# Modulation rows on GpSimd's queue, w1's first operands made ahead of the folds, and seven buffer pairs for comparisons in an FNet and mixer-MLP kernel

## The chip, the cores and the metric

The kernel runs on one core of a Trainium2 chip. The metric is the device time of one execution in microseconds (us), the median of several runs. Engines: TensorE (PE, its weight loads PEld), VectorE (DVE), ScalarE (ACT), GpSimd (POOL) and SyncE (SP); SP, ACT and POOL each issue DMA transfers from a queue of their own. On-chip memory is SBUF (128 partitions) and eight PSUM banks of 128 x 512 f32, into which PE writes.

## The reference

All is f32, with 2048 tokens of 1024 features and d_ff 3584.

```python
mod = (_silu(c) @ w_mod).reshape(c.shape[0], 6, 1, -1)
sa, ca, ga, sb, cb, gb = ...
h = _layernorm(x) * (1 + ca) + sa
# FNet: real part of a 2-D DFT, as products with given matrices
a = einsum("bsd,ed->bse", h, dft_hid_re); b = einsum("bsd,ed->bse", h, dft_hid_im)
y = einsum("ts,bse->bte", dft_seq_re, a) - einsum("ts,bse->bte", dft_seq_im, b)
x = x + ga * y
h = _layernorm(x) * (1 + cb) + sb
u = _layernorm(h)
x = x + gb * (gelu(u @ w1 + b1) @ w2 + b2)
```

The inputs are x, the four DFT matrices, w1, b1, w2, b2, the condition c and w_mod (1024 x 6144).

## The kernel before, in words

Matmuls of the DFT and of the MLP run in f16 as three passes of a high and a low half ("split": ACT makes the high half at L2340, VectorE the low half at L2350 or L2352 and w1's combined half at L2365). The function `fast` uses symmetries of DFT matrices, and it compares the matrices that it was given with those symmetries while the MLP runs; if a comparison fails, `general` computes everything again.

The stages of `fast` in order:

1. Modulation columns (sa and ca): eight loads of w_mod (1 MB each, L2457, SP), products on PE (L2500) and on VectorE (L2489 and L2491, into the sum MACC). The result is a row in PSUM. ACT copies it to SBUF, and 32 products of one column each (L2544) turn it into columns; L2551 to L2555 finish them ("mod").
2. LN1: for each of 16 tiles of x statistics (L2582, VectorE) and normalization (L2603 and L2604, ACT), then transposes on PE (L2619) in four groups over all eight banks, and from there the modulated halves (L2637, ACT) and their folds (L2641 and L2642, VectorE). The folded operands are split again (L2690 and after).
3. The hidden DFT, 297 matmuls (L2874, "hid"), in units whose results ACT and VectorE split. Among them stand the rows: ga, sb, cb and gb are wanted as rows of 1024 on all partitions, so each of four rows is a sum over eight 512 KB pieces of w_mod, loaded by SP (L2812) into a ring of three and used by two matmuls each (L2818) in banks 6 and 7. Three of the rows are then copied within SBUF to their place (L2904).
4. The sequence DFT (L2947 and L2959, "P" and "Q"), then x + ga * y, the second and third normalization (L3013 to L3045), transposes (L3063) and splits of the MLP's left operand. Its matrices are loaded by L2763 ("cop"). w1's first two groups of columns are loaded in this stage (L3309), their norms taken (L3152, an all-reduce on GpSimd at L3164), split, and stored for later blocks (L3254).
5. The MLP: 28 groups GEMM3 (L3438, 84 matmuls each, evicted by L3460, L3464, L3457) and 14 GEMM4 (L3547, 168 matmuls each, evicted and summed by L3593; the last two by L3587). From the middle on the 148 comparisons run beside them: each loads two 128 x 512 pieces on GpSimd's queue (L3369, or gathered at L3362) into one of three buffer pairs, VectorE subtracts (L3352), and ACT squares and sums (L3345). The verdict (L3429 to L3433, with an all-reduce on GpSimd at L3430) adds the sums; the program's last branch reads it.

Every engine runs its instructions in order, and that order is made before the launch by a planner: `add` and `push` append tasks with an engine, a cost, dependencies and a due time to a stream; `pick` takes the next task from the stream with the earliest due time that can start, and `need`, `force` and `emitted` put a named task and all that stands ahead of it out at once. So an edit of a due time, a dependency or a cost moves instructions on several engines. Of the names in the diff: "wru" is the use of a row load by PE, "tpd" the end of the transposes of an LN1 block, "n" the normalization of a tile, "cru" the use of a ring buffer of sequence operands, "rowe" the copy of a finished row by ACT, FP the planner's cost of an f32 matmul.

## Time and profile before

| | us |
|---|---|
| median of 3 runs | 1569.62 (1568.48 to 1572.24) |
| profiled execution | 1573.34 |
| its span | 1571.5 |
| PE busy | 1319.7 (84%) |
| DVE busy | 1121.2 (71%) |
| ACT busy | 738.6 (47%) |
| POOL busy | 254.4 (16%) |

Times in the profile count from the span's start. A row of a timeline gives the start, the busy time, the engine, the line, the operation with its operands, the number of instructions run together (x), and in brackets how long the engine had been idle before and what released it. A row of a group gives the busy time, the mean of one instruction in ns, and the idle time before such instructions with what ended most of it. A window's row gives busy times of each engine in a stretch. An f32 matmul leaves two records, so a row's 64 matmuls show as 128.

### The profile page before, as it was taken

What the parts mean: (1) busy time and instruction counts of PE and PEld (TensorE: products, weight loads), DVE (VectorE), ACT (ScalarE), POOL (GpSimd) and SP (SyncE); (2) the same over time, 40 slices, a digit from 0 to 9 for tenths busy, and PEclk for the clock granted to TensorE, in tenths of its full rate; (3) what the DMA queues carried; (4) which work ended last, traced back from release to release, by engine and by line L of the source; (5) the groups of instructions that cost most, each with busy time, mean ns of one, the idle gap of its engine ahead of it and who ended that gap; (6) DMA issues with size and microseconds to landing.
All of it is one profiled execution on the core that took longest, in us unless ns stands there. A gap on an engine that the chain in (4) does not pass through costs nothing.

```text
span 1571.5 us, 17349 instructions
## 1 busy us (share of the span) xinstructions
PE 1319.7 (84%) x6081; PEld 635.8 (40%) x6081; DVE 1121.2 (71%) x1723; ACT 738.6 (47%) x1173; POOL 254.4 (16%) x415
## 2 busy tenths in 40 slices
PE   6515899946428899999999999979999999999980
PEld 2413345624313344444444444434444444444430
DVE  6875413898984779989898899635576857676872
ACT  2724112667666568464655535135535353434412
POOL 1000000000124000000000000133243233225233
PEclk9555999968658999999999999989999999999995
DMA  9313753243479846263534437588677777675564
GB/s 371 112 27 94 245 181 136 81 141 107 152 247 197 247 148 221 98 224 122 204 137 168 149 140 312 163 276 302 230 236 260 247 227 254 224 263 184 203 147 164
DMA packets 107337, 300.18 MB, mean 191 GB/s; under 512 B 13644, under 2 KB 13644, under 8 KB 105320
## 3 DMA queue, kind: packets, MB, share of 16 engines
q1 hardware_dynamic: 75080, 194.06, 36.0%
q0 software_dynamic: 32160, 104.93, 21.6%
q8 instruction: 49, 0.80, 0.2%
q14 instruction: 48, 0.39, 0.1%
HBM read 212.43 MB, written 84.93 MB: 189 GB/s over the span
## 4 chain that ended last, share of the span: by engine, by line
PE 66%; DVE 12%; DMA 9%; issue 7%; ACT 3%; POOL 2%; SPq 1%; DVEq 0%; POOLq 0%; ACTq 0%
PE ps L3438 28%; PE ps L3547 27%; PE ps L2818 3%; DMA arena<-in_wm_dram 3%; PE ps L2874 3%; DMA arena<-in_cre_dram 2%; PE ps L2947 2%; PE ps L2959 1%; DMA arena<-in_w_dram 1%; PE ps L2500 1%; DVE arena L2365 1%; DVE arena L2350 1%; DVE arena L2352 1%; DMA arena<-in_dim_dram 1%; DMA arena<-in_cim_dram,idxs 1%
## 5 line engine op out<-in xcount | busy, mean ns | idle before, releaser
L3438 PE MATMUL ps<-arena 128*128 128x512 f16 x2352 | 521.3, 384 | 19.5 <-ACT arena L3460 16.7
L3547 PE MATMUL ps<-arena 128*128 128x512 f16 x2352 | 515.2, 381 | 12.3 <-DVE arena L3593 7.7
L3438 PEld LDWEIGHTS <-arena 128*128 128x128 f16 x2352 | 232.7, 99 | 305.7 <-issue 35.0
L3547 PEld LDWEIGHTS <-arena 128*128 128x128 f16 x2352 | 231.2, 98 | 294.0 <-issue 19.6
L3593 DVE SCALAR_TENSOR_TENSOR arena<-ps,i4c,arena 128x1024 f32<-128x1024 f32 x179 | 229.4, 1282 | 58.8 <-PE ps L3547 55.7
L3345 ACT ACTIVATE arena<-arena 128x512 f32<-128x512 f32 (+5 forms) x148 | 91.5, 619 | 191.1 <-DVE arena L3352 125.1
L2365 DVE TENSOR_TENSOR arena<-arena 128x512 f32<-128x512 f32 (+1 forms) x228 | 171.5, 754 | 5.8 <-ACT arena L3067 1.1
L2340 ACT ACTIVATE arena<-arena,shc 128x512 f16<-128x512 f32 (+1 forms) x115 | 116.6, 1016 | 93.5 <-DVE arena L2365 57.4
L2352 DVE SCALAR_TENSOR_TENSOR arena<-arena,shc 128x512 f16<-128x512 f32 (+1 forms) x115 | 129.0, 1123 | 33.1 <-ACT arena L2340 32.7
L3352 DVE TENSOR_TENSOR arena<-arena 128x256 f32<-128x256 f32 x240 | 92.3, 422 | 73.0 <-DMA arena<-in_cre_dram 38.6
L3457 ACT ACTIVATE arena<-arena,b1s,i1c 128x512 f32<-128x512 f32 x84 | 68.3, 814 | 139.0 <-DVE arena L3464 138.8
L3464 DVE TENSOR_TENSOR arena<-arena,ps 128x512 f32<-128x512 f32 x84 | 57.5, 685 | 69.0 <-PE ps L3438 68.4
L2340 ACT ACTIVATE arena<-arena,s1c 128x512 f16<-128x512 f32 (+1 forms) x70 | 60.5, 885 | 53.8 <-DVE arena L2365 40.0
L2947 PE MATMUL ps<-arena 128*128 128x256 f16 (+3 forms) x400 | 55.9, 304 | 29.7 <-DVE arena L2974 29.5
L3164 POOL PARTITION_ALL_REDUCE sums<-sums x21 | 12.8, 609 | 402.8 <-DVE sums L3160 398.0
L3369 POOL DMA_DIRECT2D arena<-in_cim_dram x99 | 54.2, 548 | 135.6 <-ACT arena L3345 133.2
L3369 POOL DMA_DIRECT2D arena<-in_cre_dram x99 | 54.3, 548 | 126.0 <-ACT arena L3345 117.5
L2619 PE MATMUL ps<-ident,arena 128*128 128x128 f32 x128 | 26.5, 378 | 53.7 <-ACT arena L2603 52.6
L2352 DVE SCALAR_TENSOR_TENSOR arena<-arena,s1c 128x512 f16<-128x512 f32 (+1 forms) x70 | 66.3, 958 | 7.1 <-ACT arena L2340 7.1
L3063 PE MATMUL ps<-ident,arena 128*128 128x128 f32 x128 | 24.7, 357 | 54.4 <-ACT arena L3053 42.8
L2818 PE MATMUL ps<-arena,scol 128*128 128x512 f32 x128 | 63.4, 640 | 8.3 <-DMA arena<-in_wm_dram 7.1
L3460 ACT ACTIVATE arena<-ps 128x512 f32<-128x512 f32 x84 | 49.5, 589 | 36.0 <-PE ps L3438 35.9
(187 smaller groups left out, 1285.4 us busy)
## 6 DMA issues: line engine op xcount, KB each, us to landing
...
```

The lines of the kernel that those rows point to most:

```text
L2340: act.activation(o[m][0], q(j), AF.Copy, **sc)
L2352: dve.scalar_tensor_tensor(o[m][1], q(j), scale, o[m][0], op0=ALU.mult, op1=ALU.subtract)
L2365: dve.tensor_tensor(q(d), q(a), q(b), op=op)
L2818: pe.matmul(bank(6 + h), scol[:, k : k + 1].to_broadcast([P, P]), FA(o + 512 * h, (1, 512)), start=k == 0, stop=k == 7,)
L2947: pe.matmul(PA(pb + o, (1, w)), l, r, start=n == 0, stop=n == len(mm_) - 1)
L3345: f = lambda: act.activation(sq(a), sq(a), AF.Square, accum_out=csum[0:pn, n : n + 1])
L3352: dve.tensor_tensor(a[:, o::2], a[:, o::2], b[:, o::2], op=op)
L3369: return lambda t: gp.dma_start(t[0:pn], v)
L3438: pe.matmul(ps.rearrange("p (k t) -> p k t", k=4), w1c[:, m, s, a, d * P : (d + 1) * P], zc(m)[:, b, :, d, :], start=(start and d == 0 and ...
L3457: act.activation(dst, src, AF.Gelu_apprx_tanh, scale=inv, bias=b1s[:, 2 * p + j : 2 * p + j + 1])
L3547: pe.matmul(t[:, j], hidc[:, c_, m, a, k * P : (k + 1) * P], w2c[:, m, c_, w], start=(start and c_ == 0 and n == 0), stop=(c_ == 1 and n = ...
L3593: lambda: dve.scalar_tensor_tensor(dst, ps[b], inv, dst, op0=ALU.mult, op1=ALU.add), kp[b],
```

## The change

It does seven things.

1. The 32 row loads (and that of b2) go from SP's queue to GpSimd's, and the row matmuls from behind LN1 to among its transposes: their due time is 45 + 12 n in place of 60. They have banks 6 and 7 to themselves and a ring of their own in the memory that holds w1's stored halves before (first loads wait for those stores). Row results go straight to their place, and the three copies at L2904 go.
2. LN1's transposes, the special columns' and the hid units share three pairs of banks in turn (`pair`), each transposed unit followed by its fold.
3. The columns: the row is copied by ACT and VectorE together, one DMA spreads it over 16 partitions, one transpose turns it, and two small products stay.
4. w1's first two groups are loaded by eight 256 KB loads ahead of w_mod, normed and split in the modulation and LN1 stages, stored by GpSimd's queue, and loaded again as 14 pieces by SP late in the hid stage and after.
5. The loads of the sequence operands (from the third on) wait for the use of row load 23, and x tiles 12 to 15 are loaded after the first row in program order.
6. Comparisons have seven buffer pairs instead of three. All of them, with the verdict, are put out before GEMM3(27); two loads of partial outputs (`load_kept`) move from after GEMM4(7) to there.
7. The planner's cost of an f32 matmul goes from 0.85 to 0.5, and addresses move.

Core of the diff:

```diff
--- before.py
+++ after.py
@@ -2049,23 +2049,24 @@
         return mk([P, n], F32, tag, bufs)
 
 
-    X0, X4, NR = 0, 29920, 4160
+    X0, X4, NR = 0, 29920, 51200
     EO, WM2, MACC, ROW, ONES = 9344, 9344, 25792, 27840, 34048
     AR, CL = 2052, 1026
     SPB = (38912, 40968)
-    DRAW = 47168
-    CRING = (42000, 49224, 50248)
-    RTMP, RFIN, WRING, GBT = (0, 1024, 2048), (51296, 52320, 53344), (3072, 4096, 5120), 6144
-    QS = (7168, 54368)
-    Y0, W0, ZT0 = 8192, 12288, 16384
+    DRAW = 47120
+    CRING = (41996, 49176, 50200)
+    ROWS = (51264, 52288, 53312)
+    WRING, GBT = ((34656, 35680, 36704), (0, 1024, 2048)), 3072
+    QS = (54852, 54336)
+    Y0, W0, ZT0 = 8832, 12928, 17024
 
     HOP, HC = 51584, 8256
-    COP = (86144, 69632)
-    AOP, AC = (94336, 77824), 4112
-    DOP, SPOP, DSP, ASP, CSP = 102592, 106752, 108832, 109888, 110944
+    COP = (86048, 69632)
+    AOP, AC = (94240, 77824), 4112
+    DOP, SPOP, DSP, ASP, CSP = 8320, 12448, 14528, 15584, 16640
 
     def junk2(key):
...
+    for g in range(2):
+        for n in (1, 2, 0, 3):
+            load(("raw1", g, n), lambda g=g, n=n: sp.dma_start(raw1(g, n), w1[g, :, PLACE.index(n), :]), cost=0.7)
     for k in range(8):
         load(("wm", k), lambda k=k: sp.dma_start(wm2(k), wm[:, k, 0 : 2 * D]), cost=2.75)
...
-        key = load(("cr", n), lambda: f(o), [("cru", n - 3)] if n > 2 else [])
+        key = load(("cr", n), lambda: f(o), ([("cru", n - 3)] if n > 2 else []) + [("wru", 23), ("tpd", 3), ("n", 15)] * (n > 1))
...
-        act.activation(
-            FA(ROW + 257, (1024, 2), (512, 2), (1, 255), pn=1), PA(MB + 511, (1024, 2), (512, 2), (-1, 255), pn=1), AF.Copy
+        act.activation(rspec[0:1], PA(MB, (1024, 2), (256, 4), pn=1), AF.Copy)
+
+    def rows_out2():
+        dve.tensor_copy(
+            FA(ROW + 257, (1024, 2), (512, 2), (1, 255), pn=1), PA(MB + 511, (1024, 2), (512, 2), (-1, 255), pn=1)
         )
-        act.activation(rspec[0:1], PA(MB, (1024, 2), (256, 4), pn=1), AF.Copy)
+
+    def rows_spread():
+        act.dma_start(FA(MACC, (1, 128), pn=16), FA(ROW, (128, 16), (1, 128), pn=1))
 
     def cols():
+        pe.transpose(PA(MB, (1, 16)), FA(MACC, (1, 128), pn=16), ident[0:16, 0:16])
         for cs in range(2):
-            for g in range(4):
-                for j in range(2):
-                    n = (cs * 4 + g) * 2 + j
-                    pe.matmul(
-                        PA(MB + n, (1, 1)), FA(ROW + 1024 * cs + 256 * g + 128 * j, (1, 128), pn=1), ones[0:1, 0:1],
-                        start=True, stop=True,
-                    )
             pe.matmul(PA(MB + 16 + cs, (1, 1), pn=4), rspec[0:1, cs], ones[0:1, 0:1], start=True, stop=True)
...
+    add("modm", "dve", 1.1, rows_out2, [("mp", 7)], "rowd", 1.0)
     add("modm", "dve", 3.2, rows_max, [("mp", 7)], "max", 1.0)
-    add("modr", "act", 3.0, rows_out, [("mp", 7)], "rowc", 1.0)
-    add("modp", "pe", 4.5, cols, ["rowc", "max"], "cols", 1.0)
+    add("modr", "act", 1.2, rows_out, [("mp", 7)], "rowc", 1.0)
+    add("modr", "act", 0.1, rows_spread, ["rowc", "rowd"], "rows16", 1.0)
+    add("modp", "pe", 2.5, cols, ["rows16", "max"], "cols", 1.0)
     add("modm", "dve", 0.8, cols_out, ["cols", "max"], "mod", 1.0)
...
-    GB = {0: (0, 1), 3: (2, 3), 1: (4, 5), 2: (6, 7)}
-    lastbank = {}
+    last = {0: [], 1: [], 2: ["mod"]}
+    nunit = [0]
+
+    def pair():
+        nunit[0] += 1
+        return (nunit[0] - 1) % 3
 
...
+                ks = [
+                    add("lnt", "pe", 0.75, lambda g=g, bk=bk, turn=turn: turn(g, bk), deps + last[s], None, due)
+                    for g, bk in ((ga_, ba), (gd_, bd))
+                ]
...
+                k2 = add("lnd", "dve", 1.5, fold, [k1, ks[1]], ("d1", bt, j, base), 1.6)
+                last[s] = [k1, k2]
...
     def row(n, j):
         for k in range(ND):
             m = ND * n + k
-            o = WRING[m % 3]
-            l = load(
-                ("wr", m), lambda o=o, k=k, j=j: sp.dma_start(FA(o, (1, 1024)), wm[:, k, j * D : (j + 1) * D]),
-                [("wru", m - 3)] if m > 2 else [("tpd", 3), ("n", 15)], stream="ld",
-            )
+            o = WRING[m > 23][m % 3]
+            was = [("wru", m - 3)] if m > 2 else [("w1s", 1, q) for q in range(7)]
+            if 24 <= m < 27:
+                was += [("tpd", 3), ("n", 15)]
+
+            def f(o=o, k=k, j=j, m=m):
+                if m < 3:
+                    need("st_w1s")
+                gp.dma_start(FA(o, (1, 1024)), wm[:, k, j * D : (j + 1) * D])
+
+            l = add("rowl", "st", 0.0, f, was, ("wr", m))
 
             def f(k=k, o=o):
                 for h in range(2):
@@ -2822,30 +2831,43 @@
 
             deps = [l]
             if k == 0:
-                deps += [("rowe", n - 1)] if n else [lastbank[6], lastbank[7]]
-            add("rowp", "pe", 2 * FP, f, deps, ("wru", m), 60.0)
+                deps.append(("rowe", n - 1) if n else "rowd")
+                deps += ["rowc", "max"]
+            add("rowp", "pe", 2 * FP, f, deps, ("wru", m), 45.0 + 12 * n)
...
+    dopk = [("dop", t, q) for t in range(2) for q in range(2)]
+    dsp_item()
+    csp_item()
+    row(0, 2)
+    for i in range(12, 16):
+        load_x(i)
+    row(1, 4)
+    row(2, 3)
+    for ch in range(4):
+        for t in range(2):
+            cop_item(t, ch)
+    row(3, 5)
+    ga_t, sb_t, cb_t = (FA(o, (1, 1024)) for o in ROWS)
+
+    rows = [("rowe", n) for n in range(3)]
...
+        s = pair()
+        bp = 1024 * s
+        deps += last[s]
+        last[s] = [("hid", n)]
...
-    for n in range(3):
-        f = lambda n=n: sp.dma_start(FA(RFIN[n], (1, 1024)), FA(RTMP[n], (1, 1024)))
-        load(("rfin", n), f, [*hidend, ("rowe", (0, 2, 1)[n])], stream="rfin", due=70.0)
-    rows = [("rfin", n) for n in range(3)]
...
+            if g < 2:
+                n = span(m).stop - span(m).start
+                v = at(135.375 + 2 * span(m).start, 1024 * n, F16).rearrange("p (m a x) -> p m a x", m=n, a=2)
+                if g:
+                    reuse("w1s", (0, m))
+            else:
+                v = w1c[:, span(m), s]
                 reuse("w1k", (g - 2, m))
...
-            store("w1k", (g, m), lambda: sp.dma_start(w1_d[g][:, span(m)], o[2]), ("w1", g, span(m).start))
+            q_, ring = (gp, "w1s") if g < 2 else (sp, "w1k")
+            store(ring, (g, m), lambda: q_.dma_start(w1_d[g][:, span(m)], o[2]), (w1res, g, span(m).start))
...
-    push_rows = [*rows, ("gbst", 0), ("gbst", 1), *hops]
     for g in range(2):
-        was = push_rows if g == 0 else [("w1", 0, m) for m in range(7)]
-        for n in range(4):
-            f = lambda g=g, n=n: sp.dma_start(raw1(g, n), w1[g, :, PLACE.index(n), :])
-            push("wl", "wl", [Task("dma", 0.75, f, was, ("raw1", g, n))], 150.0)
-        push("w", "w", w1_norm(g) + w1_tasks(g), 150.0 + 50.0 * g)
+        push("wq", "wq", w1_norm(g) + w1_tasks(g), 1.5)
+    for m in ORDER:
+        for g in range(2):
+            f = lambda g=g, m=m: sp.dma_start(w1c[:, m, g], w1_d[g][:, m])
+            load(("w1", g, m), f, [("P", 15), ("Q", 15), *hidend] if m > 3 else [("gbst", 0), ("gbst", 1)], cost=0.7, stream="wl", due=200.0)
...
-    CB = ((136, 138), (140, 142), (216, 218))
+    CB = ((136, 138), (140, 142), (216, 218), (32, 34), (36, 38), (40, 42), (44, 46))
...
-        ka, kb_ = CB[n % 3]
+        ka, kb_ = CB[n % NCB]
         a, b = at(ka, 512), at(kb_, 512)
-        free = [("chk", n - 3)] if n > 2 else []
+        free = [("chk", n - NCB)] if n >= NCB else []
...
-            if v == 7:
+            if v == 12:
+                emitted(("chk", chks[0] - 1), "verdict")
                 load_kept()
...
-                add("chkd", "dve", 2.0, verdict, [("chk", n - 1 - j) for j in range(3)], "verdict", 1e7)
+                add("chkd", "dve", 2.0, verdict, [("chk", n - 1 - j) for j in range(NCB)], "verdict", 1e7)
```

TensorE between the modulation's columns and the first hid matmul, before (L2544 and L2548 turn the row, L2619 transposes, L2656 transposes the special columns, L2874 is hid):

```order
L2544 MATMUL ps<-arena_65 128x1 x8
L2548 MATMUL ps<-arena_65,rspec_110 4x1
L2619 MATMUL ps<-ident_97,arena_65 128x128 x48
L2656 MATMUL ps<-ident_97,arena_65 4x128 x8
L2619 MATMUL ps<-ident_97,arena_65 128x128 x64
```

and now (L2549 and L2551 turn the row, L2629 transposes, L2663 the special columns, L2827 are the rows):

```order
L2549 MATMUL ps<-ident_97,arena_65 128x16
L2551 MATMUL ps<-arena_65,rspec_110 4x1 x2
L2629 MATMUL ps<-ident_97,arena_65 128x128 x40
L2827 MATMUL ps<-arena_65,scol_102 128x512 x6
L2629 MATMUL ps<-ident_97,arena_65 128x128 x8
L2663 MATMUL ps<-ident_97,arena_65 4x128 x8
L2827 MATMUL ps<-arena_65,scol_102 128x512 x6
L2629 MATMUL ps<-ident_97,arena_65 128x128 x24
L2827 MATMUL ps<-arena_65,scol_102 128x512 x4
L2629 MATMUL ps<-ident_97,arena_65 128x128 x40
L2663 MATMUL ps<-ident_97,arena_65 4x128 x8
L2827 MATMUL ps<-arena_65,scol_102 128x512 x18
```

34 of the 64 row matmuls now stand ahead of the first hid matmul; before, none did. Of the other 30, 14 stand among the first 102 hid matmuls (up to the use of row load 23) and 16 among the last 195.

GpSimd from its last memset of the start to the output stores of the sequence stage, now (L3181 is the all-reduce of w1's norms with what comes ahead of it, L3278 stores w1's halves, L3131 is an all-reduce for b1, L2821 loads the rows):

```order
L2790 MEMSET arena_65 64x1026
L3181 ISA
L3181 ISA sums_175<-sums_175 128x1
L3278 DMA fw_0_76<-arena_65 128x1024 x2
L3278 DMA fw_0_76<-arena_65 128x2048
L3278 DMA fw_0_76<-arena_65 128x1024
L3278 DMA fw_0_76<-arena_65 128x2048
L3181 ISA sums_261<-sums_261 128x1
L3278 DMA fw_1_77<-arena_65 128x1024 x2
L3278 DMA fw_1_77<-arena_65 128x2048
```

Behind these come the all-reduce for b1, two more stores and the 32 row loads. Before, that memset was followed by the all-reduce for b1 and the two stores of the last row; the first all-reduce for w1 stood in the sequence stage.

VectorE at the end of GEMM4, before (L3593 and L3587 evict, L3352 and L3410 are comparisons, L3429 begins the verdict):

```order
L3593 SCALAR_TENSOR_TENSOR arena_65<-ps,i4c_146,arena_65 128x2x512
L3352 TENSOR_TENSOR arena_65<-arena_65 128x256 x2
L3593 SCALAR_TENSOR_TENSOR arena_65<-ps,i4c_146,arena_65 128x2x512
L3587 SCALAR_TENSOR_TENSOR arena_65<-ps,i4c_146,arena_65 128x512 x2
L3352 TENSOR_TENSOR arena_65<-arena_65 128x256 x20
L3410 TENSOR_TENSOR arena_65<-arena_65 128x511
```

and at the end of GEMM4(12), now (L3617 evicts, L3434 and L3438 are the last comparison, L2353 and L2366 split w1, L3453 begins the verdict):

```order
L3434 TENSOR_TENSOR arena_65<-arena_65 1x511
L3617 SCALAR_TENSOR_TENSOR arena_65<-ps,i4c_146,arena_65 128x2x512
L3438 COPY arena_65<-arena_65 1x1
L3617 SCALAR_TENSOR_TENSOR arena_65<-ps,i4c_146,arena_65 128x2x512 x6
L2353 SCALAR_TENSOR_TENSOR arena_65<-arena_65,shc_143 128x2x512
L2366 TENSOR_TENSOR arena_65<-arena_65 128x512
```

The last comparison stood behind the last eviction of the kernel; it now has 12 evictions of GEMM4(12) behind it, then the verdict, and then GEMM3(27) and GEMM4(13).

104 lines of the change are left out of this document (42 added, 62 removed).

## The prediction

> **What bounds the kernel now.** I read the windows by stage first, then the page's costliest groups, TensorE's timeline at the borders of the stages, and last the order of the work on VectorE and GpSimd near the end. The windows give, for each stretch, its length and the busy time of PE, PEld, DVE, ACT and POOL, then the granted clock, the DMA share and GB/s:
>
> ```profile
> 0.00:49.00 49.00, 32.66 (x97) 18.12 (x98) 29.32 (x64) 15.44 (x28) 6.29 (x19) 0.88 0.83 322
> 49.00:146.00 97.00, 28.46 (x140) 22.89 (x140) 73.65 (x106) 49.19 (x73) 0.90 (x1) 0.57 0.27 72
> 146.00:260.00 114.00, 104.24 (x417) 48.99 (x416) 32.80 (x36) 20.43 (x26) 1.61 (x4) 0.92 0.54 182
> 260.00:469.00 209.00, 122.31 (x728) 82.09 (x726) 177.63 (x359) 129.87 (x204) 23.97 (x39) 0.75 0.42 143
> 560.00:1020.00 460.00, 460.00 (x2133) 208.57 (x2132) 403.70 (x547) 246.28 (x319) 13.84 (x20) 1.00 0.50 173
> 1020.00:1533.00 513.00, 495.40 (x2269) 222.86 (x2267) 338.01 (x497) 212.93 (x421) 173.91 (x283) 0.98 0.71 235
> 1533.00:1571.50 38.50, 0.00 (x0) 0.00 (x0) 11.04 (x31) 10.04 (x30) 14.30 (x23) 0.53 0.48 160
> ```
>
> Three stretches are not TensorE's bound. From 49 to 146 (LN1) PE works 28 of 97 us and VectorE 74. From 260 to 469 (the sequence stage) VectorE works 178 of 209. From 1533 on PE does nothing: only comparisons run, and they end the program. From 146 to 260 PE is busy, 104 of 114, but more than half of that is not the hidden DFT: the 64 matmuls of the rows (128 records) take 63 us.
>
> ```profile
> L2818 PE MATMUL ps<-arena,scol 128*128 128x512 f32 x128 | 63.4, 640 | 8.3 <-DMA arena<-in_wm_dram 7.1
> ```
>
> Their loads stand last in SP's queue, behind those of the sequence operands, so none of it can fill PE's idle time before 146:
>
> ```profile
> 109.01 1.25 SPq L2763 DMA_DIRECT2D arena<-in_cre_dram  x2
> ...
> 140.22 1.25 SPq L2763 DMA_DIRECT2D arena<-in_cim_dram  x2
> 141.52 38.78 SPq L2812 DMA_DIRECT2D arena<-in_wm_dram  x14
> ```
>
> **Part 1, the rows: D.** With the change 34 of the 64 row matmuls stand ahead of the first hid matmul and 30 among hid. The stretch is bounded at its start by the operands:
>
> ```profile
> 34.57 3.60 PE L2500 MATMUL ps<-arena,scol 128*128 128x512 f32 x8
> 48.37 0.23 DVE L2551 TENSOR_SCALAR mcol<-ps,m 128x16 f32<-128x16 f32 x1 [3.42 <-PE ps L2548]
> 145.58 9.92 PE L2874 MATMUL ps<-arena 128*128 128x256 f16 x42 [13.55 <-ACT arena L2659]
> 196.32 7.20 PE L2874 MATMUL ps<-arena 128*1 128x257 f16 x54
> 241.16 17.09 PE L2874 MATMUL ps<-arena 128*128 128x257 f16 x132
> 259.66 2.76 PE L2959 MATMUL ps<-arena 128*128 128x512 f16 x12 [1.42 <-DVE arena L2478]
> ```
>
> First what is late next. The modulation's columns were ready at 48.9. Now eight w1 loads (2.1 MB) go ahead of its weights: at the 322 GB/s of the first window 6.5 us. And w1's scale goes through an all-reduce on GpSimd whose library must come in first. The trace shows such gaps, "issue" or no work at all, ahead of GpSimd's special instructions:
>
> ```profile
> 8.79 0.28 POOL masks.py:199 TENSOR_SCALAR_AFFINE_SELECT ident<-ident 128x128 f32<-128x128 f32 x1 [7.86 <-issue]
> 13.72 0.96 POOL L2779 MEMSET arena<- 64x1026 f32 x1
> 1020.80 0.13 POOL L3324 IOTA sgi<- 128x1 int32 x1 [9.39 <-issue]
> 1563.93 0.40 POOL L3430 PARTITION_ALL_REDUCE csum<-csum  x1 [6.03 <-DVE csum L3429]
> ```
>
> GpSimd is free at 14.7; with a gap of 6.0 to 9.4 the first scale is there at 21 to 25. VectorE's order puts that wait, then the first w1 splits, ahead of three of the four long products of the modulation's weights, and the second scale ahead of the last of them. So those end about 50 where they ended at 38.2, and behind them come 5.5 us of statistics, the maximum, the spread through DMA (it replaces 7.3 us of one-column matmuls) and again 5.5 us of statistics: the columns are ready at about 65, 16 late. Against that, most of w1's splits and the statistics of 12 of 16 tiles are then done. VectorE's 73.65 busy us of the LN1 stretch lose about 8 of statistics and win some 12 of rest of w1, waits of small steps included: 78 to 87 us behind 65, so hid starts between 143 and 152; I take 146, as before. (All 23 us of idle time kept: 168; columns only 5 late: 134.)
>
> From there by PE's new order: up to the use of row load 23, 102 hid matmuls at 0.13 us (17.09/132) and 14 row matmuls at 0.99 (63.4/64) are 27 us, so 173; behind it 195 hid and 16 row matmuls, 25 + 16 = 41, so 214. The sequence operands' loads now wait for row load 23; they and their splits took 109.0 to about 144, 35 us, so 208 to 211: just hidden; if that chain stretches, the first sequence matmul waits for it. With 4 us for gaps it starts at 218 instead of 259.7: **D = -41.5**, between -20 (hid at 168) and -55 (hid at 134).
>
> **Part 2, w1 out of the sequence stage: C.** VectorE sets the pace there, and these are the groups that leave it (by shapes, that window):
>
> ```profile
> L2352 DVE SCALAR_TENSOR_TENSOR arena<-arena,s1c 128x1024 f16<-128x1024 f32 x4 | 5.1, 1277 | 0.0
> L2352 DVE SCALAR_TENSOR_TENSOR arena<-arena,s1c 128x512 f16<-128x512 f32 x6 | 4.4, 745 | 0.0
> L2365 DVE TENSOR_TENSOR arena<-arena 128x512 f32<-128x512 f32 x36 | 24.5, 688 | 0.6
> ```
>
> 5.1 + 4.4, 8 of the 36 combinations (5.5) and 14 small ones of about 0.15 (2.1): 17 us. On the other side stand 14 reloads of 0.5 MB on SP, 7 MB more in a stretch with a DMA share of 0.42, and x loads that no longer stand behind w1's stores: nothing on VectorE. **C = -16**, from -8 (half turns into waits for PE or ACT) to -22 (waits of the chain shrink too).
>
> **Part 3, comparisons: A and B.** The last eviction of GEMM4 and what follows it:
>
> ```profile
> 1532.86 0.75 DVE L3587 SCALAR_TENSOR_TENSOR arena<-ps,i4c,arena 128x512 f32<-128x512 f32 x1 [1.41 <-PE ps L3547]
> ...
> 1550.46 0.76 DVE L3352 TENSOR_TENSOR arena<-arena 128x256 f32<-128x256 f32 x2 [1.40 <-DMA arena<-in_dim_dram,idxd]
> 1552.57 0.76 DVE L3352 TENSOR_TENSOR arena<-arena 128x256 f32<-128x256 f32 x2 [1.34 <-DMA arena<-in_dim_dram,idxd]
> ...
> 1564.74 0.15 DVE L3433 CAST oddi<-csum 128x1 int32<-128x1 f32 x1
> ```
>
> VectorE's last operation ends at 1564.9, the last eviction at 1533.6. The change puts all comparisons and the verdict ahead of GEMM3(27); the 6.6 us from the last operation to the end of the span I leave, since the last store has to land there as well: **A = -31.3**. VectorE runs in order, and comparisons in front of evictions hold PE up (VectorE's row first, then two of PE):
>
> ```profile
> 1525.93 0.76 DVE L3352 TENSOR_TENSOR arena<-arena 128x256 f32<-128x256 f32 x2 [6.39 <-DMA arena<-in_dim_dram]
> 1052.44 15.76 PE L3438 MATMUL ps<-arena 128*128 128x512 f16 x60 [9.03 <-ACT arena L3460]
> 1527.94 4.88 PE L3547 MATMUL ps<-arena 128*128 128x512 f16 x12 [4.54 <-DVE arena L3593]
> ```
>
> The last stall, 4.54 at 1527.9, was VectorE waiting 6.39 for a comparison's load, with the evictions behind it; none stands there now: **B = -4.5**. The earlier ones (9.03 and some 4 us of short ones) I leave at 0 change, from -9 (seven pairs let loads run far enough ahead) to +25: the same 148 units must now fit in fewer microseconds. How many follows from the two large groups:
>
> ```profile
> L3438 PE MATMUL ps<-arena 128*128 128x512 f16 x2352 | 521.3, 384 | 19.5 <-ACT arena L3460 16.7
> L3547 PE MATMUL ps<-arena 128*128 128x512 f16 x2352 | 515.2, 381 | 12.3 <-DVE arena L3593 7.7
> ```
>
> 28 GEMM3 of 18.6 us and 14 GEMM4 of 36.8. GEMM3(27) and GEMM4(13) end at 1533, so GEMM4(12) ends near 1473. In VectorE's new order the last comparison has 12 of its 14 evictions behind it, 12 x 2.6 = 31 us of PE's pace: comparisons end near 1441.
>
> **Edits at nothing.** LN1's transposes take three bank pairs in turn instead of eight banks in a block, so PE waits for folds more often: VectorE's 74 us set that stretch, PE's 28 hide in it, and without that cover a wait of one fold pair (1.5 us) per unit of 16 would be 24 us, which hid at 168 already holds. The three copies of the rows, SP's last work before the w1 loads, go: nothing waited for them on PE. On GpSimd's queue the rows stand ahead of the sequence stage's output stores, which come after 218 in any case. GpSimd's all-reduce for the verdict, with a library gap of 6 to 9.4 again, has those 12 evictions, 31 us, between the last comparison and VectorE's wait: hidden; uncovered it costs VectorE up to 10 us, which the bound of +25 holds.
>
> **The sum.** 1571.5 - 41.5 - 16 - 31.3 - 4.5 = 1478 of span. The profiled execution took 1573.34, 1.8 more than its span and 3.7 more than the median of 1569.62. In the terms of the median that is 1478.2 + 1.8 - 3.7 = 1476.
>
> **The rivals.**
> 1. The early gain is swallowed. The columns at 65 push the LN1 stretch on by their 16 us, the operands' chain after row load 23 stretches, and the sequence stage starts near 260 as before. For it: 13.55 us of PE's wait at 145.58 are for ACT and VectorE, not for rows. Against it: VectorE has 23 idle us in that stretch, and half of the row work is gone from behind it. 1476 + 41.5 = 1518.
> 2. Row loads trickle. On GpSimd's queue each waits for the use three back; with issue, landing and use they give one per 2.3 us at best, and a busy VectorE may slow their issue:
>
> ```profile
> L3369 POOL DMA_DIRECT2D arena<-in_cim_dram x99 | 54.2, 548 | 135.6 <-ACT arena L3345 133.2
> 1518.56 1.20 POOL L3620 DMA_DIRECT2D out_dram<-arena  x1 [5.13 <-issue]
> ```
>
> An issue is 0.55 us in the mean and 1.20 here. Were all 32 at 1.2, 32 x 0.65 = 21 us more spread over the rows, of which those behind row 17 (15 loads, 10 us) lie on PE's path: 1486; with the sequence operands behind it some 1490. [...] The trace bears it out little: with VectorE busy 338 of 513 us the mean issue is still 0.55.
> 3. The comparisons don't fit, and it gets slower.
>
> ```profile
> 1022.12 1.83 POOL L3369 DMA_DIRECT2D arena<-in_cre_dram  x3 [0.59 <-issue]
> ```
>
> They took from 1022 to 1565, 543 us for 148 units, 3.67 each. If loads, not buffer pairs, set that pace (DMA share 0.71; indirect loads of 1 us on GpSimd), then 1022 to 1441 has room for 114, and the other 34 x 3.67 = 125 us stop VectorE, and so PE, ahead of GEMM3(27): 1476 + 125 = 1601, slower. It decides from 93/148 = 0.63 us per unit over the 2.83 that fit, that is from 3.46 on. Against it: alone, with three pairs, a unit took 2.1 us (1550.46 to 1552.57), and they were then last in everybody's order, filling gaps.
> 4. The mild form: 3.04 us per unit, 0.21 x 148 = 31 us of waits, gives back the tail: 1507. The tail is then moved and not shortened.
>
> **How the numbers follow.** Forecast with its own spread 0.62, rival 1 0.15, rival 2 0.08, rival 4 0.09, rival 3 0.05; 0.01 for no change at all by several of these together. The forecast's own range: 1476 with D -20 to -55, C -8 to -22, stalls -9 to +25, taken together as about 1450 to 1500. To leave out no more than 2 in 10 the range reaches up over rivals 2 and 4 to rival 1: 1448 to 1519. Under 0.3% (4.7 us) a measurement of this kernel tells no change. Faster 0.93, the same 0.01 to 0.02, slower 0.05.
>
> **What would show it.** Right: row matmuls between 90 and 146 on PE; the first sequence matmul near 218; a sequence stage under 200 us; no comparison on VectorE after the last eviction, and the span ending 6 to 8 us behind that. Wrong: an LN1 stretch that starts after 70 or hid after 165 (D); PE stalls of 5 us and more ahead of GEMM4(12) or GEMM3(27) with VectorE waiting for comparison loads (rivals 3, 4); SP waiting for reloads of w1 at the first GEMM3.

## The result, and the profile after

The changed kernel takes 1503.22 us (median of 4 runs, 1501.56 to 1504.36) where the kernel before took 1570.93 in the runs beside it (1568.48 to 1577.5). The ratio is 0.9562, with a 95% interval of 0.953 to 0.9594. The forecast was 1476: the direction and three of the four terms come out, and the term of the early stages, D, is half of what was expected.

The profiled execution has a span of 1502.3 us, 69.2 less than the 1571.5 before. Its windows at the new borders of the stages (length, busy time of PE, PEld, DVE, ACT and POOL, granted clock, DMA share, GB/s):

```profile
67.00:153.00 86.00, 57.25 (x195) 31.97 (x194) 71.26 (x95) 41.89 (x63) 11.17 (x21) 0.79 0.48 150
153.00:240.00 87.00, 72.95 (x360) 37.41 (x359) 33.58 (x39) 25.50 (x31) 8.62 (x18) 0.86 0.63 192
240.00:436.00 196.00, 119.74 (x729) 82.59 (x729) 162.20 (x327) 118.00 (x186) 23.03 (x37) 0.76 0.37 131
1041.00:1496.00 455.00, 454.12 (x2104) 205.58 (x2101) 321.49 (x477) 197.09 (x409) 165.95 (x259) 1.00 0.71 238
1496.00:1502.30 6.30, 0.00 (x0) 0.00 (x0) 0.00 (x0) 0.00 (x0) 0.00 (x0) 0.81 0.38 130
```

LN1's stretch now holds 57 us of PE's work where it held 28. The sequence stage has 162 us of VectorE's work where it had 178. From 1041 to 1496, with almost all comparisons in it, PE is busy 454 of 455 us. Behind the last eviction there is nothing but 6.3 us; the last two stores (L3612), issued at 1495.5 and 1496.0, landed 2.9 us after their issue.

PE's timeline at the borders, and VectorE's last eviction:

```profile
130.86 7.24 PE L2827 MATMUL ps<-arena,scol 128*128 128x512 f32 x12 [7.51 <-ACT arena L2840]
153.40 6.71 PE L2895 MATMUL ps<-arena 128*128 128x257 f16 x51
220.93 17.65 PE L2895 MATMUL ps<-arena 128*128 128x257 f16 x81 [11.41 <-DVE arena L2482]
239.99 2.76 PE L2976 MATMUL ps<-arena 128*128 128x512 f16 x12 [1.42 <-DVE arena L2482]
435.86 6.58 PE L3462 MATMUL ps<-arena 128*128 128x512 f16 x24
1031.94 9.77 PE L3462 MATMUL ps<-arena 128*128 128x512 f16 x36 [16.48 <-ACT arena L3484]
1495.23 0.75 DVE L3611 SCALAR_TENSOR_TENSOR arena<-ps,i4c,arena 128x512 f32<-128x512 f32 x1 [0.54 <-PE ps L3571]
```

| stretch | before | after | difference | forecast |
|---|---|---|---|---|
| start to the first sequence matmul (D) | 259.7 | 240.0 | -19.7 | -41.5 |
| from there to the first GEMM3 (C) | 209.4 | 195.9 | -13.5 | -16 |
| from there to the last eviction's end (B) | 1064.6 | 1060.1 | -4.5 | -4.5 |
| from there to the end of the span (A) | 37.9 | 6.3 | -31.6 | -31.3 |

The four differences make -69.3. So 22 of the 24 to 27 us that are missing against the forecast lie ahead of the first sequence matmul, and the rows show where. Of hid's 297 matmuls the last 81 waited 11.4 us for VectorE, and then took 17.65 us, 0.218 each, where 132 took 17.09 before, 0.129 each. In that stretch PE's granted clock was 0.56:

```profile
221.00:239.00 18.00, 17.57 (x81) 9.15 (x81) 5.14 (x7) 3.19 (x6) 1.21 (x4) 0.56 0.24 89
```

VectorE, in its order, stood at the split of the last piece of the sequence operands (there are eight pieces, of two 256 KB loads each). ACT's half of that split waited for the loads, and VectorE's ended at 220.3:

```profile
215.49 1.13 ACT L2479 ACTIVATE arena<-arena 128x1024 f16<-128x1024 f32 x1 [7.57 <-DMA arena<-in_cim_dram]
219.05 1.23 DVE L2482 SCALAR_TENSOR_TENSOR arena<-arena 128x1024 f16<-128x1024 f32 x1 [1.18 <-ACT arena L2479]
```

Of the operands' loads, the medians from issue to landing, after (170 to 245), were:

```profile
arena<-in_cre_dram SPq DMA_DIRECT2D x8, 256.0 KB, 9.2
arena<-in_cim_dram SPq DMA_DIRECT2D x8, 256.0 KB, 8.4
```

and before (105 to 146):

```profile
arena<-in_cre_dram SPq DMA_DIRECT2D x6, 256.0 KB, 4.6
arena<-in_cim_dram SPq DMA_DIRECT2D x6, 256.0 KB, 4.0
```

Three questions follow, which the experiments take up: whether the comparisons' gain is their own and what gives it; what stretches the operands' chain; and whether the slow last 81 matmuls are the clock's doing.

### The profile page after: what moved, and what is told of

It is laid out like the page before. It is cut to its first block, busy times and chain, and to the rows that moved or that the text cites. A ratio compares the mean times of both kernels' runs of the same rounds, so it can differ in the third digit from the quotient of the medians.

```text
span 1502.3 us, 17318 instructions
## 1 busy us (share of the span) xinstructions
PE 1305.8 (87%) x6050; PEld 626.7 (42%) x6050; DVE 1119.6 (75%) x1724; ACT 733.5 (49%) x1172; POOL 279.5 (19%) x458
## 4 chain that ended last, share of the span: by engine, by line
PE 69%; DVE 7%; issue 7%; DMA 5%; ACT 4%; POOL 2%; SPq 0%; POOLq 0%; ACTq 0%; DVEq 0%
PE ps L3571 33%; PE ps L3462 30%; PE ps L2964 2%; PE ps L2976 2%; PE ps L2895 2%; DMA arena<-in_cre_dram 1%; DMA arena<-in_wm_dram 1%; DMA arena<-in_cim_dram 1%; DVE arena L2366 1%; PE ps L2827 1%; DVE arena L2351 1%; POOL fzc L3105 1%; DMA arena<-in_w_dram 1%; DVE arena L2482 1%; DVE arena L3062 1%
## 5 line engine op out<-in xcount | busy, mean ns | idle before, releaser
L3462 PE MATMUL ps<-arena 128*128 128x512 f16 x2352 | 518.7, 383 | 28.5 <-ACT arena L3484 22.7
L3571 PE MATMUL ps<-arena 128*128 128x512 f16 x2352 | 511.9, 380 | 4.5 <-ACT arena L3607 4.5
L3617 DVE SCALAR_TENSOR_TENSOR arena<-ps,i4c,arena 128x1024 f32<-128x1024 f32 x179 | 229.6, 1283 | 100.7 <-PE ps L3571 97.3
L2366 DVE TENSOR_TENSOR arena<-arena 128x512 f32<-128x512 f32 (+1 forms) x228 | 171.5, 754 | 9.3 <-ACT arena L3084 5.3
L2353 DVE SCALAR_TENSOR_TENSOR arena<-arena,shc 128x512 f16<-128x512 f32 (+1 forms) x115 | 128.8, 1122 | 32.1 <-ACT arena L2341 31.8
L3376 DVE TENSOR_TENSOR arena<-arena 128x256 f32<-128x256 f32 x240 | 88.5, 423 | 25.5 <-DMA arena<-in_cre_dram 25.5
L3080 PE MATMUL ps<-ident,arena 128*128 128x128 f32 x128 | 28.4, 395 | 72.5 <-ACT arena L3070 55.3
L3181 POOL PARTITION_ALL_REDUCE sums<-sums x21 | 12.7, 603 | 407.6 <-DVE sums L3177 395.5
L2827 PE MATMUL ps<-arena,scol 128*128 128x512 f32 x128 | 62.9, 634 | 14.7 <-ACT arena L2840 7.5
L2353 DVE SCALAR_TENSOR_TENSOR arena<-arena,s1c 128x512 f16<-128x512 f32 (+1 forms) x70 | 66.3, 959 | 9.2 <-ACT arena L2341 9.2
L3169 ACT ACTIVATE ps<-arena 128x1024 f32<-128x1024 f32 x52 | 52.9, 1018 | 24.7 <-DMA arena<-in_w_dram 12.9
L2353 DVE SCALAR_TENSOR_TENSOR arena<-arena,s2c 128x1024 f16<-128x1024 f32 x49 | 62.0, 1280 | 1.3 <-ACT arena L2341 1.2
```

What stands on the lines that cost most here:

```text
L2353: dve.scalar_tensor_tensor(o[m][1], q(j), scale, o[m][0], op0=ALU.mult, op1=ALU.subtract)
L2366: dve.tensor_tensor(q(d), q(a), q(b), op=op)
L2827: pe.matmul(bank(6 + h), scol[:, k : k + 1].to_broadcast([P, P]), FA(o + 512 * h, (1, 512)), start=k == 0, stop=k == 7,)
L3376: dve.tensor_tensor(a[:, o::2], a[:, o::2], b[:, o::2], op=op)
L3462: pe.matmul(ps.rearrange("p (k t) -> p k t", k=4), w1c[:, m, s, a, d * P : (d + 1) * P], zc(m)[:, b, :, d, :], start=(start and d == 0 and ...
L3571: pe.matmul(t[:, j], hidc[:, c_, m, a, k * P : (k + 1) * P], w2c[:, m, c_, w], start=(start and c_ == 0 and n == 0), stop=(c_ == 1 and n = ...
```

## The experiments

Experiments without an interval are one profiled execution and one time each. One warning holds for all of these: the changed kernel's early stages ran unchanged in two of the experiments (three pairs, and stores first), and their first sequence matmul came at 238.8 and 233.8 against 240.0. A difference of up to 6 us there, by itself, tells nothing; what tells is the wait, the clock or the landing inside it.

**1. The comparisons' part alone, in the kernel before.**

```diff
-    CB = ((136, 138), (140, 142), (216, 218))
+    CB = ((136, 138), (140, 142), (216, 218), (32, 34), (36, 38), (40, 42), (44, 46))
...
-            if v == 7:
+            if v == 12:
+                emitted(("chk", chks[0] - 1), "verdict")
                 load_kept()
```

> The kernel before with the comparisons' part alone: seven buffer pairs, all comparisons and the verdict ahead of GEMM3(27), the two loads of partial outputs moved there too. Theory: this part is independent of the rest and is worth what the two traces show for it, 31.6 us of tail and about 4.5 us of waits, so about 1570.9 - 36 = 1535 us, the span ending 6 to 7 us behind the last eviction. Rival: the comparisons fit only because the changed kernel reaches the MLP earlier or with another order; then PE waits appear ahead of GEMM4(12) and the time is 1545 or more.

Measured: 1534.06 us (1533.05 to 1538.07) against 1571.02, ratio 0.9769 (95% interval 0.9716 to 0.9822), a gain of 37. The theory holds: this part does not need the rest. PE's waits from 990 to the end, of this run:

```profile
PE ps L3439 <- ACT arena L3461: 16.1, 2, 15.3
PE ps L3439 <- DVE arena L3465: 0.7, 1, 0.7
```

The waits at the end are gone, and the first one, at the comparisons' start, has grown from 9.0 to 15.3, as it grew to 16.5 in the changed kernel. That growth comes with this part, and within it with the seven pairs: with three pairs in the changed kernel (experiment 2) the wait there is 9.3.

**2. Three pairs again, in the changed kernel.**

```diff
-    CB = ((136, 138), (140, 142), (216, 218), (32, 34), (36, 38), (40, 42), (44, 46))
+    CB = ((136, 138), (140, 142), (216, 218))
```

> The changed kernel with three buffer pairs again, comparisons and verdict still ahead of GEMM3(27). Theory P: seven pairs are what lets 148 units fit in about 420 us; a unit's loads take 1.1 us to issue and 4 to 5 us to land, its work 2 us, so three pairs give one unit per 2.6 us at best and PE waits for evictions behind late comparisons: 10 to 40 us more than 1503. Theory Q: the place of the verdict alone does it: within 4 us of 1503.

Measured: 1554.71 us, 51 more. One wait, ahead of GEMM3(27), where all comparisons must be done, is 53.9 us:

```profile
1493.49 15.41 PE L3462 MATMUL ps<-arena 128*128 128x512 f16 x60 [53.93 <-ACT arena L3484]
```

So theory P holds, and the price lies above its range of 10 to 40. The comparisons fail to fit, as in the prediction's rival 3, but for another cause: rival 3 took the loads to set the pace and not the buffer pairs, and here the pairs set it. By an estimate from this run and experiment 1 (51 us lost against 37 gained), the place of the verdict alone would have cost more than it gained; the seven pairs are what lets 148 units fit (in the changed kernel they went from the first load at 986.6 to the last subtraction at 1413.5, 2.88 us each).

**3. The first two x loads of the second normalization behind the sequence operands.**

```diff
-        deps = [("turn", 2 * b - 4 + n) for n in range(2)] if b > 1 else hops
+        deps = [("turn", 2 * b - 4 + n) for n in range(2)] if b > 1 else [*hops, *copk]
```

> The changed kernel with the first two loads of x for the second normalization (1 MB each) behind the last sequence operand instead of among them. Theory D (the operands' loads land late because they share DMA with rows, x and w1's reloads, 8.6 us in the median against 4 to 4.6 before): 2 MB at 270 GB/s are 7 us less in that chain; PE's wait of 11.4 us ahead of the last 81 hid matmuls falls to about 4, the first sequence matmul comes at 230 to 235 instead of 240, the time at 1494 to 1498. Rival R (the ring of three buffers and the splits set the chain's pace): the first sequence matmul stays within 2 us of 240, the time at 1503.

Measured: 1498.35 us; first sequence matmul at 235.4. VectorE's last operand split:

```profile
213.56 1.23 DVE L2482 SCALAR_TENSOR_TENSOR arena<-arena 128x1024 f16<-128x1024 f32 x1 [1.19 <-ACT arena L2479]
```

It ended at 214.8 instead of 220.3, and PE's waits there were 5.1 us for VectorE and 2.7 for a row load instead of 11.4. The gain at the first sequence matmul, 4.6, is inside the spread named above. And the edit did more than take 2 MB away. In the changed kernel the first of these x loads stands in SP's queue ahead of the operands; with it gone, the first three pieces were loaded 58 us earlier, and the DMA share from 172 to 210 fell from 0.90 to 0.52:

```profile
114.57 1.39 SPq L2774 DMA_DIRECT2D arena<-in_cre_dram  x2
```

```profile
172.00:210.00 38.00, 32.93 (x163) 16.51 (x161) 11.52 (x13) 12.61 (x15) 1.59 (x3) 0.84 0.52 151
```

The other five pieces took from 184.7 to 214.8, 30.1 us, where they took from 187.7 to 220.3, 32.6, with all those bytes beside them. So this run doesn't decide between D and R: of the 5.5 us, 2.5 are the five pieces' own and 3.0 their earlier start. In experiment 4 the x loads stayed at 171, the first three pieces came early all the same (115.9), the other five took 37.7 us, and the last split ended at 214.6.

**4. The first finished row copied away at once.**

```diff
-            add("rowa", "act", 1.1, lambda: act.activation(FA(ROWS[0], ...), src, ...), [("wru", 7), "mod", ("tpd", 3)], ("rowe", 0), due)
+            add("rowa", "act", 1.1, lambda: act.activation(FA(RT0, ...), src, ...), [("wru", 7), "mod"], ("rowe", 0), due)
+            add("rowa2", "act", 1.1, lambda: act.activation(FA(ROWS[0], ...), FA(RT0, ...), AF.Copy), [("rowe", 0), ("tpd", 3), ("n", 15)], ("rowf", 0), due)
...
-            add("rowa", "act", 1.1, f, [("wru", 15)], ("rowe", 1), due)
+            add("rowa", "act", 1.1, f, [("wru", 15), ("tpd", 3), ("n", 15)], ("rowe", 1), due)
...
```

> The changed kernel with the first finished row copied to a free place at once, and to its final place when LN1's tiles are read. So the rows behind it need not wait for LN1's end (PE waited 7.5 us at 130.9 for that copy, and GpSimd's queue 26.6 us for PE). Theory: hid starts when its operands are ready, at 146 to 148 instead of 153.4, row load 23 is used some 8 to 12 us earlier, the operands' chain and the first sequence matmul come 7 to 12 us earlier (228 to 233), the time at 1491 to 1496. Rival: the chain of operands is bound by DMA sharing, which grows when rows and operands come together: first sequence matmul at 237 to 240, time 1500 to 1503.

Measured: 1503.56 us. It missed:

```profile
145.68 6.66 PE L2828 MATMUL ps<-arena,scol 128*128 128x512 f32 x8 [7.24 <-ACT arena L2844]
```

The wait of 7.5 us behind the first row became one of 7.2 behind the second, whose place also lies in memory that LN1 reads to its end, and whose copy waits for that end. Hid began at 152.2. The first sequence matmul at 234.3 is inside the spread, and PE still waited 10.5 us for VectorE, at 209.9. Removing one row's share of the wait moved it.

**5. A fourth buffer for the operands.**

```diff
-    CRING = (41996, 49176, 50200)
+    CRING = (41996, 49176, 50200, 40968)
...
-        o = CRING[n % 3]
+        o = CRING[n % 4]
...
```

> The changed kernel with a fourth buffer for loads of the sequence operands (where the special columns of class 1 have been, once these are split). Eight items then go through in two rounds instead of three. Theory C (the chain of loads and splits behind row load 23, some 13 us a round, holds the last five hid units): the last split ends at 205 to 212 instead of 220, PE's wait of 11.4 us falls to 0 to 4, the last hid matmuls run faster for it, the first sequence matmul comes at 223 to 232, the time at 1488 to 1497. Rival D (all is bound by bytes: DMA share 0.90 from 172 to 210): landing times grow as the ring does, first sequence matmul at 237 to 240, the time at 1500 to 1503.

Measured: 1503.65 us. The last split ended at 219.5, within 1 us of the 220.3 with three buffers:

```profile
218.29 1.23 DVE L2482 SCALAR_TENSOR_TENSOR arena<-arena 128x1024 f16<-128x1024 f32 x1 [1.19 <-ACT arena L2479]
```

The first sequence matmul came at 237.1, and PE's wait of 10.6 us stood at 204.5, ahead of an earlier unit. Theory C falls: two rounds took as long as three, so a fourth buffer alone doesn't shorten the chain. Rival D's first sequence matmul came, but landings that grow with the ring are seen in one of the two medians only: 9.8 and 7.3, where they were 9.2 and 8.4. What sets the chain's length was not tried further.

**6. PE kept busy ahead of the wait.**

```diff
-                for i, (l, r) in enumerate(mm_):
-                    pe.matmul(...)
+                for _ in range(6 if n == 12 else 1):
+                    for i, (l, r) in enumerate(mm_):
+                        pe.matmul(...)
```

> The changed kernel with the matmuls of the hid unit ahead of PE's wait (15 of them) done six times over with the same result, which is 75 more matmuls, about 10 us of work without use. Theory G (the last 81 hid matmuls took 17.6 us instead of 10.5 because PE had idled 11 us and its granted clock was 0.56): the idle time falls to 1 to 4 us, the clock stays at 0.9 or more, the 81 take 10.5 to 13 us, the first sequence matmul comes at 232 to 236, so 4 to 8 us earlier for doing more. Rival W (the units were slow because each waited for banks or operands): the 81 still take 17 to 18 us, first sequence matmul at 239 to 242.

Measured: 1496.06 us, with 75 matmuls more; the first sequence matmul came at 232.8. PE's row, and the window of the last 81:

```profile
220.91 10.43 PE L2896 MATMUL ps<-arena 128*128 128x257 f16 x81 [1.31 <-DVE arena L2482]
```

```profile
221.00:232.00 11.00, 10.33 (x81) 6.64 (x81) 5.11 (x7) 3.65 (x7) 1.22 (x4) 1.00 0.46 170
```

The 81 began at the same time as in the changed kernel (220.9), waited for the same split, and took 10.43 us instead of 17.65, at a granted clock of 1.00 instead of 0.56. So theory G holds: these 7 us go with the granted clock, which was 0.56 behind a wait of 11.4 us and 1.00 behind one of 1.31. That the repetition is a sure remedy is not shown: version a below has the same 75 and the 81 were slow again.

How long the matmuls stayed slow behind a wait differed from run to run. The same 81 took 17.65 us behind 11.4 us in the changed kernel, 17.29 behind 10.5 in experiment 2, and 12.32 behind 10.4 in experiment 7, of which some 4.6 us slow (an estimate: what 0.218 for the first and 0.129 for the others makes of 81). Slow matmuls followed much shorter waits as well: 36 hid matmuls took 8.36 us behind 2.49 (experiment 9), where 36 took 4.85 behind 1.21 here, and the 81 took 16.50 behind 2.55 (version a). What ended the slow stretches no run shows.

**7. The four accumulating stores ahead of the comparisons.**

```diff
                 push("fin", "fin", final_tasks(0, range(4, 8)), due[4, 7])
+                need("fin")
                 chk_start()
```

> The changed kernel with four accumulating stores to the output put on GpSimd's queue ahead of the comparisons' start instead of among the first comparison loads. Theory Q (the longest PE wait of the MLP, 16.5 us near 1032, is a comparison's load standing in GpSimd's queue behind those four stores, with VectorE waiting 15.4 us for it): the wait falls to 0 to 6 us, the time at 1487 to 1495. Rival L (the wait comes from the gap of 9.2 us ahead of the index instructions and the first loads' own landing): 10 us and more of it stay, the time at 1497 to 1504.

Measured: 1494.98 us, 8.2 less. Of these 6.2 lie ahead of the first sequence matmul, where the code is the same and the last 81 hid matmuls took 12.32 us instead of 17.65. At the comparisons' start 11.8 us of wait stay, and VectorE's row says why:

```profile
998.49 0.15 DVE L3349 TENSOR_SCALAR sgi<-sgi 128x1 int32<-128x1 int32 x1 [17.76 <-POOL sgi L3348]
```

The index instructions stood behind the four stores, the last of which was issued at 989.4, with a gap of 8.05 us on top in which GpSimd waited for nothing that the trace shows. Rival L is nearer than theory Q, though the time lies below its range, for the early stages. The first comparison's load, issued 10 us behind the last of the four stores, was used 4 us after its issue (999.6 to 1003.6).

**8. w1's first loads behind the modulation's.** The two loops that issue them change places.

> The changed kernel with w1's eight first loads behind those of the modulation's weights instead of ahead. The columns should be ready at 48 to 58 instead of 61 to 66. Theory S (lateness of the columns costs nothing by itself, since VectorE then does the same work in another order, and w1's stores hold the row loads back): first hid matmul at 150 to 160, first sequence matmul at 238 to 250, the time at 1500 to 1514. Rival M (the late columns are what D lacks): hid starts at 140 or earlier, first sequence matmul at 228 or earlier, the time at 1492 or less.

Measured: 1501.16 us. The columns were ready 9 us earlier:

```profile
56.84 0.18 DVE L2554 TENSOR_SCALAR mcol<-ps,m 128x16 f32<-128x16 f32 x1
```

Hid began at 150.3 and the first sequence matmul came at 240.2. Theory S holds: the columns' lateness, which the prediction priced and found covered, costs nothing that shows beyond the spread.

**9. Row loads on SP's queue.**

```diff
-                gp.dma_start(FA(o, (1, 1024)), wm[:, k, j * D : (j + 1) * D])
+                sp.dma_start(FA(o, (1, 1024)), wm[:, k, j * D : (j + 1) * D])
```

> The changed kernel with the row loads issued by SP again, everything else as changed (order of PE, banks, ring). On SP's queue the loads of x tiles 12 to 15 then stand behind the first three row loads, and the sequence operands' loads behind row load 26, each waiting for PE's use three back. Theory (the queue of its own matters because SP's loads would wait behind row loads): LN1's last transposes come 5 to 15 us later than 121 us, the sequence operands' loads start later than 173, the first sequence matmul at 245 to 260, the time at 1508 to 1522. Rival (what counts is the order on PE, not the queue; GpSimd issues at 0.53 us each, SP at 0.6): first sequence matmul within 3 us of 234 to 240, the time at 1495 to 1504.

Measured: 1509.28 us. SP's rows, and PE's:

```profile
79.08 1.49 SPq L2821 DMA_DIRECT2D arena<-in_wm_dram  x2
80.66 2.03 SPq L2453 DMA_DIRECT2D arena<-in_x_dram  x4
96.50 77.25 SPq L2821 DMA_DIRECT2D arena<-in_wm_dram  x23
...
92.49 1.11 PE L2629 MATMUL ps<-ident,arena 128*128 128x128 f32 x4 [12.41 <-DVE arena L2647]
245.62 2.76 PE L2976 MATMUL ps<-arena 128*128 128x512 f16 x12 [1.42 <-DVE arena L2482]
```

x tiles 12 to 15 were loaded at 80.7 instead of 71.8, LN1's last transposes ended 5.7 us later (127.4 for 121.7), and the first sequence matmul came at 245.6, behind all three executions of the changed kernel's early stages (233.8 to 240.0). The theory holds at the low end of its range: by these single executions the queue of their own is worth some 6 us in LN1. Another row of PE bears on the slow matmuls: behind a wait of 2.49 us, 36 hid matmuls took 0.232 us each.

```profile
201.27 8.36 PE L2895 MATMUL ps<-arena 128*128 128x257 f16 x36 [2.49 <-DVE arena L2482]
```

**10 and 11. Two versions with the comparisons' start cleared.** Both have the stores first and the index instructions during GEMM4(6):

```diff
             gemm3(g, {13: reload, 27: lasts}.get(g))
+            if g == 13:
+                chk_index()
```

Version a also repeats the hid unit as in experiment 6. Version b instead has the x loads and w1's reloads behind the operands.

> The changed kernel with three edits: the hid unit ahead of PE's wait done six times (as tried, 7 us earlier first sequence matmul), the four stores ahead of the comparisons, and the comparisons' index instructions on GpSimd during GEMM4(6), behind the last all-reduce for w1 (near 899), so that their library gap of 8 to 9 us is over before the comparisons start; in the run with the stores first VectorE waited 17.8 us for the first index. Expected: PE's wait at the comparisons' start falls from 11.8 and 16.5 us to 0 to 6; 1503 - 7 - 11 to 16 = 1480 to 1485 us, ratio to before 0.943 +- 0.004. If the first comparisons' loads themselves hold VectorE, some 10 us of wait stay and the time is 1490.

> The same two edits at the comparisons' start, and in place of repeated matmuls the first loads of x for the second normalization and w1's reloads behind the last sequence operand. If fewer bytes beside the operands' loads are worth as much as a warm clock (last split at 214.8 instead of 220.3 with x alone later), first sequence matmul at 230 to 234 and a time within 4 us of the other version, 1480 to 1487; if the clock decides, 3 to 8 us slower than the other version.

Measured: a 1493.55 us (1491.94 to 1499.63), ratio to before 0.9521 (0.9487 to 0.9555); b 1498.11 (1493.12 to 1499.39), 0.9543 (0.9505 to 0.958). The intervals overlap, so which of the two is faster is not settled, and both overlap that of the changed kernel (0.953 to 0.9594), so neither is shown to be faster than it. Version a missed its 1480 to 1485 and version b its 1480 to 1487, mostly for one reason. VectorE and PE in version a:

```profile
1009.37 0.76 DVE L3379 TENSOR_TENSOR arena<-arena 128x256 f32<-128x256 f32 x2 [15.69 <-DMA arena<-in_cre_dram]
...
1014.84 22.24 PE L3465 MATMUL ps<-arena 128*128 128x512 f16 x96 [12.79 <-DVE arena L3491]
```

The index was ready at 910, and the wait was still there: the first load, issued behind four accumulating stores, was used 12 us after its issue (997.3 to 1009.4). PE waited 12.8 us there in version a and 13.1 in version b. Version a's profile shows a second miss: after a wait of only 2.55 us the last 81 hid matmuls took 16.50 us, at a clock of 0.60:

```profile
221.21 16.50 PE L2896 MATMUL ps<-arena 128*128 128x257 f16 x81 [2.55 <-DVE arena L2482]
```

In version b the first sequence matmul came at 237.2 and not at 230 to 234, although the x loads and w1's reloads stood behind the operands: PE waited 4.8 us for a split at 198.8 and 2.9 for a row load at 220.3, much as in experiment 3 (5.1 and 2.7).

**12. Comparisons started three evictions later.** Version a with the hid unit done seven times, and:

```diff
+            if g == 15:
+                chk_start()
+                chk_tasks()
...
             if v == 6:
                 push("fin", "fin", final_tasks(0, range(4, 8)), due[4, 7])
-                chk_start()
-                chk_tasks()
...
```

> The better version of before (hid unit ahead of PE's wait repeated, now seven times; stores first; index instructions early) with the start of the comparisons put three evictions later in program order, behind GEMM3(15). In that version VectorE still waited 15.7 us for the first comparison's load, issued behind four accumulating stores, 12 us from issue to use. Theory T (the loads' own time behind the stores is what holds VectorE, wherever the stores stand; only comparisons that start later hide it): PE's wait of 12.8 us falls to 0 to 5, no new waits ahead of GEMM3(27), time 1481 to 1487. Rival: the planner's model starts them too early again, or 2.7 us a unit is more than loads allow, and waits of 8 us or more stay: 1489 to 1496.

Measured: 1478.74 us (1476.96 to 1481.92), ratio to before 0.9427 (0.938 to 0.9474). PE's rows at the former wait, and in hid:

```profile
977.94 36.42 PE L3465 MATMUL ps<-arena 128*128 128x512 f16 x168
...
220.58 8.57 PE L2896 MATMUL ps<-arena 128*128 128x257 f16 x66 [0.58 <-DVE arena L2482]
```

GEMM3(14) and GEMM3(15) run through as one block of 168, where 12.8 us of wait stood, and the comparisons still fit ahead of GEMM3(27): no wait stands there. Theory T holds: a later start covers the loads' time. Hid's last units ran at a granted clock of 1.00 (220 to 234; 66 in 8.57 us, 0.130 each). This version beats both kernels: 92.6 us less than the kernel before in the same runs, and its ratio's interval lies wholly below the changed kernel's (0.938 to 0.9474 against 0.953 to 0.9594).

## Why the prediction was right, and where it was off

**A, the tail, -31.3: right.** Measured -31.6; what follows the last eviction is 6.3 us, as the 6.6 that was left standing. Experiment 1, with nothing else changed, leaves 6.8 us behind the last eviction.

**B, comparisons on PE's path, -4.5: right as a sum, and that is luck.** The late waits went (7.7 us in all, not only the 4.5). The first wait grew from 9.0 to 16.5, which the bound of +25 held but the value, 0, did not. And the matmuls' own busy time fell by 5.9 us (521.3 + 515.2 before, 518.7 + 511.9 after), which no term had. The granted clock was 0.98 from 1020 to 1533 before and is 1.00 from 1041 to 1496 now; whether that comes from the fewer waits was not tried by itself. The step that failed here is "the earlier ones I leave at 0". VectorE's row shows what it waited for:

```profile
1021.92 0.76 DVE L3376 TENSOR_TENSOR arena<-arena 128x256 f32<-128x256 f32 x2 [15.37 <-DMA arena<-in_cre_dram]
```

That load was issued at 1009.5, behind four accumulating stores, which stood between the first comparison loads in the trace of before as well. With the stores ahead of all comparison loads, the wait was for the index instructions (experiment 7) or, with these done, still for the first load (version a). Of the orders tried only a later start of the comparisons covers it (experiment 12). Rival 3, which needed 3.46 us a unit, did not come, because a unit took 2.88.

**C, the sequence stage, -16: right, 2.5 us too much.** VectorE's busy time fell from 177.6 to 162.2, 15.4 for the 17 that was counted, and the stage by 13.5.

**D, the early stages, -41.5: right in sign and mis-sized by 22.** Its steps one by one:

- The gap ahead of the first all-reduce (6.0 to 9.4) was 7.36, and that all-reduce ran at 22.0 (21 to 25). The prediction put such gaps down to a library; the trace shows the idle time ("issue") and not what fills it. The columns (L2554) were there at 66.2, and the small steps behind them ended by 66.7 (65). GpSimd's and VectorE's rows of the timeline:

```profile
22.02 0.40 POOL L3181 PARTITION_ALL_REDUCE sums<-sums  x1 [7.36 <-issue]
66.00 0.20 DVE L2554 TENSOR_SCALAR mcol<-ps,m 128x16 f32<-128x16 f32 x1
```

- "Hid starts between 143 and 152; I take 146": its operands were ready at 146.5, but it began at 153.4. PE's order has 18 row matmuls ahead of it, and these stood until 130.9 for the copy of the first row, which waits for LN1's end. The prediction set hid's start by the operands alone and read no wait for the rows there. This left PE, with all that stands ahead of the last 81 matmuls, at 209.5 instead of 203.6 (the forecast 214 less 81 matmuls of 0.129): 5.9 us.
- "The sequence operands' loads now wait for row load 23": they didn't. They began at 172.9, as forecast (173), but PE used row load 23 from 178.8 on. That wait (item 5 of the change) orders the planner's list only. On the chip the loads stood in SP's queue behind the first x load of the second normalization, which waited 94.6 us for VectorE's split of the hid operands (L2724). That the start came out right is luck. SP's rows, its wait, and PE's use:

```profile
172.47 0.38 SPq L3008 DMA_DIRECT2D arena<-in_x_dram  x1
172.94 1.39 SPq L2774 DMA_DIRECT2D arena<-in_cre_dram  x2
```

```profile
SPq L3008 <- DVE arena L2724: 94.6, 1, 94.6
```

```profile
178.83 1.98 PE L2827 MATMUL ps<-arena,scol 128*128 128x512 f32 x4
```

- "They and their splits took 109.0 to about 144, 35 us, so 208 to 211: just hidden" is the step that failed most. They took 47, from 172.9 to 220.3. The 35 us hold only six of the eight pieces, since in the kernel before the first two had been loaded at 61:

```profile
61.28 1.40 SPq L2763 DMA_DIRECT2D arena<-in_cre_dram  x2
62.77 1.24 SPq L2763 DMA_DIRECT2D arena<-in_cim_dram  x2
```

  At 35/6 = 5.8 us a piece, eight are 47: the term was mis-sized by two pieces. Price: the 11.4 us wait. The loads also landed later than before (8.4 to 9.2 us in the median instead of 4.0 to 4.6), in a stretch with a DMA share of 0.90 from 172 to 210. That this alone made the 47 is not shown: at a share of 0.52 (experiment 3) the last five pieces took 30.1 us, against 32.6. What makes a piece take some 6 us in a quiet stretch and in a busy one stays open.
- The price of 0.13 us a hid matmul did not hold behind the 11.4 us wait. The last 81 took 0.218 each: 7.2 us more, which experiment 6 took back. The trace of before had shown it: 42 matmuls in 9.92 us, 0.236 each, behind a wait of 13.55. The prediction quoted that row and used the other one.
- Of the 4 us of margin for gaps 1.4 were used: -2.6.

5.9 + 11.4 + 7.2 - 2.6 = 21.9, which is the whole miss of D.

**The rivals.** Rival 1 (the early gain swallowed) came half true: the sequence stage started at 240 and not near 260, by the operands' chain, which its second clause names, and not by the late columns (experiment 8). Rival 2 (row loads trickle) did not come: an issue took 0.53 to 0.54 us in LN1's stretch, although VectorE was busy 71 of 86 us beside it. With the same loads on SP's queue the kernel took 1509.28 us (experiment 9).
